# The attention steps of units 8 to 22 moved forward by 0.45 to 0.7 slots in a slot-ordered kernel

## Chip, core and metric

The kernel runs on one core of one Trainium2 chip. The metric is the device time of one execution in microseconds, the median of several runs. The engines in question are TensorE (PE, with its weight loads PEld), VectorE (DVE), ScalarE (ACT) and the DMA queue that SyncE issues (SP). Each works through its own list of instructions in the order in which the program put them there.

## What is computed

Three layers follow each other, for 4 sequences of 768 tokens:

```python
# 1. a linear-attention recurrence, 8 heads of 48
y[:, :, t] = einsum(r[t], state + (u * k[t]) outer v[t])
state = w[t] * state + k[t] outer v[t]
# 2. a dense layer on all 3072 tokens, 384 -> 2048 -> 384
h = x @ w_in
g = h * tanh(softplus(h))
x = g @ w_out
# 3. a greedy gate (8 experts, 384 tokens each), then relu(x @ w1[e]) @ w2[e]
```

## The kernel before

**Tiling.** The recurrence is cut into 24 units (n = 0 to 23); a unit is one chunk of 64 tokens of two sequences, 12 chunks to a pair of sequences. Two units make a group of 256 tokens (g = 0 to 11), and the dense layer works group by group: its first product `mm1` in 8 parts j of 256 hidden columns each (18 matmuls of 256 columns into one of two `Hp` buffers), its second product `mm2` in a stream of small pieces of 3 matmuls.

**Slots.** All work of layers 1 and 2 is a list of events, each with a time in slots, and the program is written out in the sorted order of these times (line 799). There are 96 slots, one `mm1` part to a slot: part j of group g stands at 8g + j + 0.7, and two or three pieces of `mm2` follow at .275 of the next slot. A step of unit n with the offset o stands at 4n - 13 + o (line 737). The offsets come from the table `'u'` of `CFG`, and from `'un'` for single units. The times are no clock: they only decide which instruction stands ahead of which in each engine's list. So four slots, a *half group*, hold one unit, four parts of `mm1` and four stretches of `mm2`.

**Steps of a unit**, with their lines and what they ask of the engines:

- `att0` (390, 393): DVE scan `E`, then the product `rk`.
- `bon1` (422) and `bon2` (428): PE, each followed by a move (`bT`, `bt`) on ACT; `bon2` ends with the DVE product `Dt` (433).
- `inv` (401, 402, 404): ACT table load, Ln and Exp, then DVE `nt`.
- `r1` (412): one DVE product.
- `k1` (439, 442): two DVE instructions that leave the scaled k in the unit's tile `T`.
- `K` (475): four PE transposes of `T`, then the move `kn`. The last chunk of a pair (units 11 and 23) has none.
- `A1` (458, 464): PE products of `T` with `T` and with the state, then the DVE `copy_predicated` (466).
- `S` (493, 500, 502): the new state, on PE and then two or three DVE instructions; none for units 11 and 23, two for unit 12.
- `y` (515, 373, 522): PE, then ACT moves the output to `xg`, and DVE writes its low part. After an odd unit SP packs `xg` with six small DMAs (528); the first `mm1` part of the next group reads them.

**The dense layer's activations**, between the steps: after each `mm1` part ACT reads `Hp` twice (613 `es`, then `hs` by the helper at 373); an `Hp` buffer is free again after `hs`. Twice a group, at the end of a half, ACT runs Arctan (620); 1.6 slots later Sin in two halves q = 0, 1 (630), each followed by a DVE product (631). Sigmoid, Ln/Exp and Sin need three different ACT tables, so every half group has three table loads. On DVE two products `g` (644) follow.

After slot 96 come the gate and the experts, which the change doesn't touch.

Of the kernel before, what the change touches and what calls it, by code (L numbers as in the profile page):

```python
# [25 lines left out]
 'ogT': [7.4, 8.45, 9.9, 10.25, 10.95, 11.85, 12.55, 12.75],  # L26
 'ogM': [8.15, 9.35, 10.2, 10.9, 11.35, 11.95, 12.75, 13.95],
 'u': {'att0': -0.5,
       'bon1': 1.4,
       'bon2': 2.4,  # L30
       'r1': 2.7,
       'k1': 3.175,
       'K': 4.91,
       'A1': 5.52,
       'S': 7.29,
       'y': 7.3,
       'inv': 2.67},
 'un': {0: {'att0': -17.25,
            'inv': -16.75,
            'r1': -16.55,  # L40
# [36 lines left out]
            'y': 6.5},  # L77
        4: {'K': 4.96,
            'A1': 4.82,
            'S': 6.99,  # L80
            'y': 7.0,
            'att0': -0.0,
            'bon1': 0.87,
            'bon2': 3.15,
            'inv': 2.57,
            'r1': 2.6,
            'k1': 3.2},
        5: {'y': 7.46,
            'att0': -1.5,
            'bon1': 2.0,  # L90
            'bon2': 4.6,
# [1 line left out]
            'r1': 3.7,  # L93
            'k1': 4.3,
            'K': 5.9,
            'A1': 6.2,
            'S': 7.45},
        6: {'y': 7.41,
            'K': 5.66,
            'A1': 6.67,  # L100
# [10 lines left out]
            'inv': 2.77,  # L111
            'r1': 2.8,
            'k1': 3.4,
            'K': 5.26,
            'A1': 5.87,
            'S': 7.29,
            'y': 7.3},
        22: {'K': 4.46},
        23: {'K': 4.3, 'A1': 6.0, 'y': 7.1}},
 'rate': [(9, 0), (80, 194), (82, 200), (85, 216), (89, 218), (93, 234), (99, 258)],  # L120
 'close_cv': 15.0,
 'close_att': 86.65,
# [1212 lines left out]
```

## Time and profile before

| | us |
|---|---|
| median of 3 runs | 858.98 (857.58 to 864.3) |
| the profiled execution | 864.1 |
| its span | 862.4 |
| PE busy | 762.9 (88%) |
| PEld busy | 523.1 (61%) |
| DVE busy | 530.4 (62%) |
| ACT busy | 508.6 (59%) |
| PE idle before L610 (`mm1`), of which until a DMA of `xg` / until ACT's `hs` | 34.6, of which 18.4 / 14.4 |

The shares are means over stages: loading and weight conversion up to about 150 us, the steady groups from about 150 to 530 us, the gate until about 645 us, the experts after that. The profile page names for each group of instructions the idle time of its engine just before it and what ended that idle time.

### The profile page before, as it was taken

To read this page: it belongs to the slowest core of one execution; us is meant where nothing else is said; L and a number is where in the kernel's file an instruction comes from. 1 tells how busy PE (TensorE), PEld (TensorE's weight loads), DVE (VectorE), ACT (ScalarE), POOL (GpSimd) and SP (SyncE) were. 2 spreads that over 40 slices of the span, in tenths; PEclk is the share of its full clock that TensorE was granted. 3 is DMA by queue.
4 is the path that set the end of the run, shared out by engine and by line. 5 is a ranking of instruction groups with operands and counts; after the bars stand their busy time and mean duration, and the time that the engine had idled before them with its cause. 6 is when DMAs were issued, how large, how long until landed. Compare 5 with 4: busy or idle time off the path is not lost. (4 is left out here: it accounts for less than half of the span.)

```text
span 862.4 us, 20166 instructions
## 1 busy us (share of the span) xinstructions
PE 762.9 (88%) x8819; PEld 523.1 (61%) x8819; DVE 530.4 (62%) x933; ACT 508.6 (59%) x728; POOL 66.9 (8%) x104
## 2 busy tenths in 40 slices
PE   7774879898898889888899999999959999999996
PEld 4462657576676667666676767555536566555564
DVE  6699885656666767586666642677766533455520
ACT  2349888687887878676778887211005543455521
POOL 1100000000000000000000001000010332222311
PEclk9697889899999999999999999999969999999998
DMA  7860511221232204221221000400244434555200
GB/s 282 235 203 14 148 37 43 49 51 40 52 75 53 56 6 85 51 52 39 53 47 25 11 14 11 165 20 20 55 150 162 141 133 175 189 192 178 71 28 27
DMA packets 22220, 74.12 MB, mean 86 GB/s; under 512 B 4496, under 2 KB 13072, under 8 KB 20080
## 3 DMA queue, kind: packets, MB, share of 16 engines
q1 hardware_dynamic: 19056, 63.35, 25.4%
q0 software_dynamic: 3072, 9.44, 3.5%
q8 instruction: 71, 1.16, 0.6%
q14 instruction: 21, 0.17, 0.1%
HBM read 62.15 MB, written 9.44 MB: 83 GB/s over the span
## 5 line engine op out<-in xcount | busy, mean ns | idle before, releaser
L610 PE MATMUL Hp<-xg,wi 128*128 128x256 f16 x1728 | 214.0, 278 | 34.6 <-DMA xg<-xg 18.4
L658 PE MATMUL X<-wo,g 128*128 128x392 f16 (+1 forms) x1152 | 217.7, 334 | 0.3 <-ACT wT L373 0.3
L610 PEld LDWEIGHTS <-wi 128*128 128x128 f16 x1728 | 167.1, 100 | 69.9 <-issue 26.1
L658 PEld LDWEIGHTS <-g 128*128 128x128 f16 x1152 | 109.5, 99 | 64.9 <-issue 4.5
L1180 PE MATMUL Hp<-xe,a 128*128 128x384 f16 (+1 forms) x612 | 101.0, 317 | 6.4 <-DVE hT L1185 5.2
L613 ACT ACTIVATE es<-Hp 128x512 f32<-128x512 f32 x96 | 58.2, 607 | 80.4 <-PE Hp L610 80.2
L1197 PE MATMUL X<-a,hT 128*128 128x384 f16 x576 | 97.2, 326 | 0.0
L631 DVE TENSOR_TENSOR hs<-hs,es 128x1024 f32<-128x1024 f32 x48 | 56.8, 1222 | 58.7 <-ACT es L630 58.6
L1180 PEld LDWEIGHTS <-a 128*128 128x128 f16 x612 | 57.8, 98 | 48.3 <-issue 14.4
L1197 PEld LDWEIGHTS <-hT 128*128 128x128 f16 x576 | 56.3, 98 | 34.8
L1185 DVE SCALAR_TENSOR_TENSOR hT<-Hp,hT 128x384 f16<-128x384 f32 x64 | 35.4, 554 | 46.8 <-ACT hT L1184 46.8
L1126 DVE SCALAR_TENSOR_TENSOR a<-stg,a 128x1024 f16<-128x1024 f32 (+4 forms) x56 | 59.7, 1067 | 3.2 <-ACT a L1123 2.7
L644 DVE TENSOR_TENSOR g<-hs,g 128x1024 f16<-128x1024 f32 x48 | 58.0, 1244 | 4.8 <-ACT g L373 4.2
L1200 ACT ACTIVATE or<-X 128x384 f32<-128x384 f32 x24 | 11.8, 490 | 81.0 <-issue 60.7
L1123 ACT ACTIVATE a<-stg 128x1024 f16<-128x1024 f32 (+4 forms) x56 | 51.1, 926 | 8.1 <-DMA stg<-in_w_dram 8.1
L373 ACT ACTIVATE hs<-Hp 128x512 f32<-128x512 f32 x91 | 55.3, 608 | 0.0
L630 ACT ACTIVATE es<-es,right 128x1024 f32<-128x1024 f32 x48 | 52.6, 1141 | 0.3
L1184 ACT ACTIVATE hT<-Hp 128x384 f16<-128x384 f32 x64 | 31.4, 490 | 32.9 <-PE Hp L1180 31.8
L1162 DVE SCALAR_TENSOR_TENSOR xe<-cn,xe 128x384 f16<-128x384 f32 x24 | 13.3, 555 | 60.9 <-ACT xe L1161 60.8
L373 ACT ACTIVATE x1o<-X 128x384 f32<-128x384 f32 x19 | 9.4, 495 | 70.0 <-issue 58.5
L620 ACT ACTIVATE es<-es 128x2048 f32<-128x2048 f32 x24 | 46.6, 1940 | 0.1
L1147 POOL DMA_INDIRECT xr<-x_dram,idx x24 | 29.2, 1215 | 114.7 <-DVE idx L1098 106.1
(196 smaller groups left out, 948.3 us busy)
## 6 DMA issues: line engine op xcount, KB each, us to landing
stg<-in_w_dram SPq DMA_DIRECT2D x16, 1536.0 KB, 7.3
T<-in_rkw_dram SPq DMA_DIRECT2D x42, 289.5 KB, 5.0
v<-in_v_dram SPq DMA_DIRECT2D x24, 192.0 KB, 3.4
raw<-in_w_out_dram SPq DMA_DIRECT2D x6, 768.0 KB, 4.8
x_dram<-x1o SPq DMA_DIRECT2D x48, 96.0 KB, 2.2
wo<-in_w_in_dram SPq DMA_DIRECT2D x4, 768.0 KB, 9.4
raw<-in_w_in_dram SPq DMA_DIRECT2D x2, 768.0 KB, 8.3
g<-in_w_in_dram SPq DMA_DIRECT2D x2, 768.0 KB, 11.2
```

The costliest lines, as they stand in the source:

```text
L373: nc.scalar.activation(dst, src, AF.Copy, scale=scale)
L610: nc.tensor.matmul(h[:, fi, :], wi[:, a, kk, f * P:(f + 1) * P], xg[g][:, b, kk, :], start=(n == 0), stop=(n == 3 * KD - 1))
L613: nc.scalar.activation(es[g, hf][:, 2 * q:2 * q + 2, :], h, AF.Sigmoid, scale=-1.0 / (SX * SWI))
L620: nc.scalar.activation(e, e, AF.Arctan)
L630: nc.scalar.activation(e, e, AF.Sin, scale=-2.0, bias=right)
L631: nc.vector.tensor_tensor(h, h, e, op=ALU.mult)
L644: (nc.vector if on_v("glo", 2 * H_ + q) else nc.gpsimd).tensor_tensor(gt[:, 1, sl], h, gt[:, 0, sl], op=ALU.subtract)
L658: nc.tensor.matmul(x, gt[:, a, ff, m * P:(m + 1) * P], wo[:, b, f, 0:n], start=(f == 0 and i == 0), stop=(f == NF - 1 and i == 2))
L1123: nc.scalar.activation(dst[:, 0], src, AF.Copy, scale=sc_)
L1126: nc.vector.scalar_tensor_tensor(dst[:, 1], src, sc_, dst[:, 0], op0=ALU.mult, op1=ALU.subtract)
L1180: nc.tensor.matmul(ps[:, cs], a1[:, a, kk, f * P:(f + 1) * P], x[:, b, kk, cs], start=(n == 0), stop=(n == 3 * KD - 1))
L1197: nc.tensor.matmul(ps, h[:, a, f, ms], a2[:, b, f, :], start=(n == 0), stop=(n == 3 * NF2 - 1))
```

## The change

In the table for all units, nine steps stand 0.45 to 0.7 slots earlier and `att0` stays:

```diff
-       'bon1': 1.4,
-       'bon2': 2.4,
-       'r1': 2.7,
-       'k1': 3.175,
-       'K': 4.91,
-       'A1': 5.52,
-       'S': 7.29,
-       'y': 7.3,
-       'inv': 2.67},
+       'bon1': 0.9,
+       'bon2': 1.9,
+       'r1': 2.25,
+       'k1': 2.7,
+       'K': 4.4,
+       'A1': 5.0,
+       'S': 6.59,
+       'y': 6.6,
+       'inv': 2.2},
```

Units 0 to 7 have tables of their own. Of these, unit 4 has `S` and `y` 0.1 slots earlier, unit 5 `A1` by 0.2 and `S` and `y` by 0.56, unit 7 `K`, `A1`, `S` and `y` by 0.26 to 0.5. Unit 22 loses its own `K` (4.46, now 4.4), unit 23 keeps its own `K` and `A1` (4.2 and 5.0, before 4.3 and 6.0) and takes `y` from the table. Nothing is added or removed: the instructions are the same, in another order. The changed file is one line shorter, so every line number above 115 is one less in it.

What this does to the lists is shown for unit 18 (its tile is `T_88`, its scan `E_134`), in the half group of `mm1` parts 4 to 7 of group 7.

DVE, from unit 18's `nt` on; `hs<-hs,es` are the two Sin products, `S_135` and `xg` belong to unit 17's `S` and `y`, and the next unit's scan follows. Before:

```order
L631 TENSOR_TENSOR hs<-hs,es 128x1024 x2
L404 TENSOR_TENSOR nt<-inv,E_134 128x512
L412 TENSOR_TENSOR T_88<-T_88,E_134 128x512
L439 SCALAR_TENSOR_TENSOR inv<-nt,inv 128x512
L442 SCALAR_TENSOR_TENSOR T_88<-inv,T_88 128x512
L371 TENSOR_SCALAR x1o<-X 128x384
L662 TENSOR_SCALAR V<-X 128x8
L500 TENSOR_TENSOR S_135<-S_138,Y 128x4x48 x2
L502 TENSOR_TENSOR S_135<-S_135,E_137 128x8x48
L522 SCALAR_TENSOR_TENSOR xg<-A,xg 128x4x64 x2
L390 SCALAR_TENSOR_TENSOR E_137<-T_89,first 128x520
```

and after the change:

```order
L403 TENSOR_TENSOR nt<-inv,E_134 128x512
L411 TENSOR_TENSOR T_88<-T_88,E_134 128x512
L630 TENSOR_TENSOR hs<-hs,es 128x1024
L499 TENSOR_TENSOR S_135<-S_138,Y 128x4x48 x2
L501 TENSOR_TENSOR S_135<-S_135,E_137 128x8x48
L521 SCALAR_TENSOR_TENSOR xg<-A,xg 128x4x64 x2
L630 TENSOR_TENSOR hs<-hs,es 128x1024
L438 SCALAR_TENSOR_TENSOR inv<-nt,inv 128x512
L441 SCALAR_TENSOR_TENSOR T_88<-inv,T_88 128x512
L370 TENSOR_SCALAR x1o<-X 128x384
L661 TENSOR_SCALAR V<-X 128x8
L389 SCALAR_TENSOR_TENSOR E_137<-T_89,first 128x520
```

The Sin products moved behind `nt` and `r1`; `S` and the low part of `xg` moved ahead of the second of them, and `k1` of unit 18 (`inv`, then `T_88`) now stands behind all of these.

ACT in the same half, from the move `bt` of unit 18 on; `es<-es,right` are the Sins, `inv` is Ln and Exp, `xg` is unit 17's `y`. Before:

```order
L373 ACTIVATE bt<-Y 128x8
L629 ACT_TABLE_LOAD
L630 ACTIVATE es<-es,right 128x1024 x2
L400 ACT_TABLE_LOAD
L401 ACTIVATE inv<-E_134 128x512
L402 ACTIVATE inv<-inv 128x512
L613 ACT_TABLE_LOAD
L613 ACTIVATE es<-Hp 128x512
L373 ACTIVATE hs<-Hp 128x512
L373 ACTIVATE xg<-A 128x4x128
```

and after the change:

```order
L372 ACTIVATE bt<-Y 128x8
L399 ACT_TABLE_LOAD
L400 ACTIVATE inv<-E_134 128x512
L401 ACTIVATE inv<-inv 128x512
L628 ACT_TABLE_LOAD
L629 ACTIVATE es<-es,right 128x1024
L372 ACTIVATE xg<-A 128x4x128
L629 ACTIVATE es<-es,right 128x1024
L612 ACT_TABLE_LOAD
L612 ACTIVATE es<-Hp 128x512
L372 ACTIVATE hs<-Hp 128x512
```

Ln and Exp moved ahead of the Sins, and the move to `xg` ahead of the second Sin; the table loads are three in both.

PE around the transposes `K` of unit 18, the last matmul ahead of them and the first behind. Before:

```order
L610 LDWEIGHTS wi
L610 MATMUL Hp<-xg,wi 128x256
L475 MATMUL Y<-ident,T_88 128x128 x4
L658 LDWEIGHTS g
L658 MATMUL X<-wo,g 128x392
```

and after the change:

```order
L657 LDWEIGHTS g
L657 MATMUL X<-wo,g 128x392
L474 MATMUL Y<-ident,T_88 128x128 x4
L609 LDWEIGHTS wi
L609 MATMUL Hp<-xg,wi 128x256
```

The transposes moved from behind the half's last `mm1` part to ahead of it, behind the stretch of `mm2` that precedes that part.

## Rows read from the trace of the kernel before

**Rows 1.** Busy time in one whole group: stretch, engines, granted clock, DMA.
```profile
core 0: us, PE busy (x) PEld busy (x) DVE busy (x) ACT busy (x) POOL busy (x), PEclk, DMA share, GB/s
231.70:269.50 37.80, 33.05 (x480) 24.97 (x473) 25.25 (x36) 31.55 (x44) 0.00 (x0) 1.00 0.24 52
```

**Rows 2.** Waits of PE from 150 to 505 us: total, times, longest.
```profile
PE Hp L610 <- DMA xg<-xg: 18.4, 11, 2.9
PE Hp L610 <- ACT hs L373: 14.4, 14, 1.7
PE Y L422 <- DVE rk L393: 2.0, 5, 0.7
```

**Rows 3.** PE in time: start, duration, line, idle before; one half group.
```profile
367.70 2.14 PE L610 MATMUL Hp<-xg,wi 128*128 128x256 f16 x18
...
380.20 2.12 PE L610 MATMUL Hp<-xg,wi 128*128 128x256 f16 x18 [1.18 <-ACT hs L373]
...
382.17 0.60 PE L475 MATMUL Y<-ident,T 128*128 128x128 f32 x4
...
382.60 1.66 PE L658 MATMUL X<-wo,g 128*128 128x392 f16 x9
...
389.04 2.87 PE L610 MATMUL Hp<-xg,wi 128*128 128x256 f16 x18 [2.91 <-DMA xg<-xg]
```

**Rows 4.** ACT in the same half group, same columns.
```profile
369.87 0.60 ACT L613 ACTIVATE es<-Hp 128x512 f32<-128x512 f32 x1 [2.32 <-PE Hp L610]
...
371.47 0.18 ACT L373 ACTIVATE bt<-Y 128x8 f32<-128x8 f32 x1 [1.00 <-PE Y L428]
...
371.67 1.28 ACT L629 ACT_TABLE_LOAD   x1
...
372.96 2.19 ACT L630 ACTIVATE es<-es,right 128x1024 f32<-128x1024 f32 x2
...
376.46 0.63 ACT L401 ACTIVATE inv<-E 128x512 f32<-128x512 f32 x1
...
379.07 0.60 ACT L613 ACTIVATE es<-Hp 128x512 f32<-128x512 f32 x1
...
379.56 0.59 ACT L373 ACTIVATE hs<-Hp 128x512 f32<-128x512 f32 x1
```

**Rows 5.** DVE in the same half group, same columns.
```profile
374.14 2.36 DVE L631 TENSOR_TENSOR hs<-hs,es 128x1024 f32<-128x1024 f32 x2 [1.77 <-ACT es L630]
...
379.00 0.68 DVE L439 SCALAR_TENSOR_TENSOR inv<-nt,inv 128x512 f32<-128x512 f32 x1
...
379.72 0.69 DVE L442 SCALAR_TENSOR_TENSOR T<-inv,T 128x512 f32<-128x512 f32 x1
...
380.87 0.61 DVE L500 TENSOR_TENSOR S<-S,Y 128x192 f32<-128x192 f32 x2
...
381.99 0.75 DVE L522 SCALAR_TENSOR_TENSOR xg<-A,xg 128x256 f16<-128x256 f32 x2
...
382.65 1.23 DVE L390 TENSOR_TENSOR_SCAN E<-T,first 128x520 f32<-128x520 f32 x1
...
383.80 0.66 DVE L393 TENSOR_TENSOR rk<-T 128x512 f32<-128x512 f32 x1
```

**Rows 6.** PE, the transposes of unit 22, same columns.
```profile
461.02 0.66 PE L475 MATMUL Y<-ident,T 128*128 128x128 f32 x4 [0.65 <-DVE S L500]
```

**Rows 7.** 3.4 us behind each PE wait over 1.8 us, columns of rows 1.
```profile
154.90:158.30 3.40, 3.40 (x46) 1.92 (x47) 0.00 (x0) 2.79 (x4) 0.00 (x0) 0.50 0.00 0
165.15:168.55 3.40, 3.40 (x57) 2.60 (x50) 3.33 (x8) 1.88 (x2) 0.00 (x0) 0.50 0.22 65
272.20:275.60 3.40, 3.40 (x27) 2.64 (x27) 0.09 (x1) 1.36 (x4) 0.00 (x0) 1.00 0.93 195
310.45:313.85 3.40, 3.40 (x27) 2.63 (x27) 0.10 (x1) 1.38 (x4) 0.00 (x0) 1.00 0.00 0
349.45:352.85 3.40, 3.40 (x14) 1.85 (x13) 0.00 (x0) 1.08 (x2) 0.00 (x0) 0.50 0.91 193
390.45:393.85 3.40, 3.40 (x15) 1.89 (x13) 0.69 (x1) 0.60 (x1) 0.00 (x0) 0.50 0.33 72
```

More of the change, by code (lines that the diff above doesn't have):

```diff
@@ L79 @@
             'A1': 4.82,
-            'S': 6.99,
-            'y': 7.0,
+            'S': 6.89,
+            'y': 6.9,
             'att0': -0.0,
@@ L87 @@
             'k1': 3.2},
-        5: {'y': 7.46,
+        5: {'y': 6.9,
             'att0': -1.5,
@@ L95 @@
             'K': 5.9,
-            'A1': 6.2,
-            'S': 7.45},
+            'A1': 6.0,
+            'S': 6.89},
         6: {'y': 7.41,
@@ L113 @@
             'k1': 3.4,
[L114 to L119, printed above, removed]
+            'K': 5.0,
+            'A1': 5.4,
+            'S': 6.79,
+            'y': 6.8},
+        23: {'K': 4.2, 'A1': 5.0}},
  'rate': [(9, 0), (80, 194), (82, 200), (85, 216), (89, 218), (93, 234), (99, 258)],
```

## Prediction

> **What bounds the kernel now.** I read the busy time by group first. In a whole group of 37.80 us PE is busy for 33.05, ACT for 31.55 and DVE for 25.25 [rows 1]: PE sets the pace but stands still for some 4 us a group, and ACT has little room behind it. The waits of PE come next [rows 2]. From 150 to 505 us it waits 18.4 us for the packing DMAs of `xg`, at the first `mm1` part of a group, 14.4 us for ACT to free an `Hp` buffer, at the last part of a half group, and 2.0 us for `rk`: 34.8 us together. The timeline of PE, ACT and DVE over one half group then gives the places and durations [rows 3 to 5]; I count time there from the half's first `mm1` part, at 367.70. The last `mm1` part is reached at 11.32 and waits 1.18 for `hs`, and the next group's first part waits 2.91 for `xg` [rows 3]. These two kinds of wait are what the change can win. Last I looked at TensorE's granted clock behind the longest waits: PE waited over 1.8 us six times after 150 us, and behind four of them 3.4 us ran at 0.50, the 1.2 GHz level, though PE was busy throughout; behind the other two the clock stayed at 1.00, which is 2.4 GHz [rows 7]. One such drop costs half of 3.4, 1.7 us.
>
> **The change, step by step.** Nothing is added, so only waits and the clock can move the time.
>
> *`xg` comes early enough.* Follow ACT in the new order. `es` of the half's first part starts 2.17 after that part [rows 3, 4]; successive reads of `Hp` start 0.49 apart, so `bt` follows `hs` at 3.15. From `bt` to the table load is 0.20, the load 1.29, and Ln, Exp and the next load take 2.61 (376.46 to 379.07) [rows 4]. The first Sin starts at 7.25. On DVE its product starts 1.18 later, at 8.43; the two products take 2.36, so one takes 1.18; then come `S`, 1.12 to the low part of `xg`, and that part, 0.75 [rows 5]. It ends at 11.48; before it ended at 382.74, which is 15.04. In the old half 6.30 went from there to the matmul that read the last packed piece. That gives 17.8, and PE comes to the next group no sooner than 19.5 (below). So the 18.4 us go. SP's list is not in the way: the unit load and the `v` load stand ahead of the packing as before.
>
> *`K` comes too early.* The transposes of unit n now stand ahead of the half's last `mm1` part, and they read what `k1` of the same unit writes. What PE does before it reaches them is the same set of matmuls as before it reached that part, so PE is there at 11.32. On DVE `k1` now stands behind the first Sin product, `S`, `xg` and the second Sin product: the latter starts 0.66 after the second half of `xg` was begun (381.99 to 382.65), at 11.39, and takes 1.18; `k1` takes 1.41 (379.00 to 380.41) [rows 5]. `k1` ends at 13.98, where before it ended at 12.71 and was read at 14.47 [rows 3, 5]. So PE stands for 2.7 us, with everything behind the transposes: the last `mm1` part, `bon1`, `A1`, a stretch of `mm2`, the next half. That chain closes on itself, for the next `bt` waits for the next `mm1` part. The wait for `Hp` disappears in it: `hs` would free its buffer at 12.3 (the second Sin ends at 9.9, the table load takes 1.29, `es` and `hs` 1.08). The wait for `rk` disappears too. From 14.0 the transposes (0.43), the part (1.97) and what follows to the next half (3.53, less some rk wait) [rows 3] give the 19.5 used above.
>
> That a transpose placed there does hold PE is seen once: unit 22's stand ahead of the `mm1` part already, and PE waits 0.65 for DVE at them [rows 6]. The Trainium skill ("TensorE: Matmul & The Clock Gate", The mechanism) says that only weight loads may overtake, and that matmuls start and end in program order. By that rule the waiting transposes hold the part behind them, and the trace agrees in the 0.65 us; if matmuls could overtake too, the first rival's time would come out.
>
> *Counting the stalls.* Units 9, 10 and 14 to 22 have the full one: 11 x 2.7 = 29.7. Unit 13 follows a unit whose `S` has one instruction less (about 0.5): 2.2. Unit 12 follows one without `S`: 1.6. At unit 8, `S` and `xg` of unit 7 still stand behind `k1`: 0.9. Unit 11 has no transposes; there the wait for `hs` stays (1.0), and `bon1` waits for `rk`, which ends 1.15 + 0.66 after `k1` [rows 5], at 15.8, instead of 14.3: 1.5. Sum 36.9, against 34.8 removed: **+2.1 us**. The waits that the change was to remove are replaced almost exactly.
>
> *The clock.* Three of the four drops stand behind waits for `xg` and go: -5.1. The one at 165 us is behind another wait and stays. Twelve new stalls of 2.2 us or more come. No row says which of them is followed by a drop: below, none; above, all twelve, 20.4. Four of six waits over 1.8 us were, and the new ones are mostly longer, so I take 8 of 12: **+13.6**.
>
> The Trainium skill ("TensorE: Matmul & The Clock Gate", What's actually happening) puts the cost of running slow until the clock rises at under 1% of a typical kernel's span. By that, an estimate, the drops after 150 us would cost at most 8.6 us here instead of the 15.3 of nine drops, and the sum would be 868. The profile before agrees with it (four drops, 6.8 us); the sum goes by the count of stalls.
>
> *Units 4, 5, 7 and the end.* The earlier `y` of units 5 and 7 serves groups 2 and 3, whose waits are in the 18.4 already. Up to 150 us and in the gate and experts no row lets me expect a change: 0, or a microsecond or two to either side.
>
> **Sum.** 864.1 + 2.1 - 5.1 + 13.6 = 874.7 for the profiled execution. That execution lies 5.1 us above the median of the runs, 858.98. The clock drops that the sum takes away are of the kind that may differ between executions; a median run that has three fewer gives 859.0 + 2.1 + 13.6 = 874.7 as well. Without that, the median would be some 5 us lower. I take 874.
>
> **The rivals.**
>
> *The transposes don't wait (faster).* If `k1` ended by 11.3 instead of 14.0, or if the `mm1` part overtook the waiting transposes, only the waits for `hs` would be left, 12.3 - 11.3 = 1.0 in each of 16 halves. Then 34.8 - 16 = 18.8 us are won, and the three drops: 864.1 - 18.8 - 5.1 = 840. It decides from a lead of 2.7 us on DVE. Against it: four instructions stand in between, and ACT gives the first Sin no sooner than 8.4. For it: unit 22's transposes, placed alike before, waited only 0.65 [rows 6], though there with `k1` ahead of `S` and `xg`. 0.13.
>
> *They wait, but the clock holds.* 864.1 + 2.1 - 5.1 = 861. For it: two of six waits left the clock at 1.00 [rows 7]. Against it: behind the longest wait, the 2.91 us at 389.04 [rows 3], it fell. 0.27.
>
> *More than that.* Every stall is followed by a drop, or DVE, which then has work from 8.4 to beyond 18 without a pause, delays `bon1` and `A1` too: 881 and over. 0.10.
>
> *`xg` is late all the same.* Then a stall would have to be shorter, since both wait in the same chain; it changes the place of the wait, not the time, and is within the forecast.
>
> **How the numbers follow.** Forecast 0.50, at 874; clock holds 0.27, at 861; faster 0.13, at 840; worse 0.10. The range leaves out the fast rival and part of the worst: its low end is 861 less 0.5 us at each of twelve stalls (855), its high end 881 and 2 us (883). A change of 1% is about what a measurement of this kernel can tell from none, 850.4 to 867.6. Faster: the first rival, 0.13. Same: the second and the lower tail of the forecast, 0.33. Slower: 0.54.
>
> **What would show it.** Right: PE's waits for `xg` shrink from 18.4 to under 3, those for `hs` nearly vanish, and a wait of the transposes (line 474 after the change) for DVE's `T` appears, 12 to 14 times, some 2.7 each; half groups of 19.5 us instead of 18.4 without the `xg` wait (389.04 - 2.91 - 367.70); new stretches at 0.50 behind some of them. Wrong: no such wait, or one of under 1 us (then `k1` was earlier than worked out, and the first rival holds); or the waits there, but few stretches at 0.50 (the second). Most fragile is the number of drops, 1.7 us each.

## The result

| | before | after |
|---|---|---|
| median (us) | 860.97 (857.58 to 864.3, 4 runs) | 872.25 (871.41 to 873.53, 4 runs) |
| ratio, 95% interval | 1 | 1.0133 (1.0084 to 1.0181) |
| the profiled execution (us) | 864.1 | 872.8 |
| its span (us) | 862.4 | 871.1 |

The changed kernel is slower by 1.3%. Below are PE's waits from 150 to 520 us, to set beside [rows 2]. Line numbers are one less than in the kernel before, so 474 are the transposes, 421 is `bon1`, 609 `mm1`, and 492 the first product of `S`:

```profile
PE Y L474 <- DVE T L441: 16.5, 7, 2.7
PE Y L474 <- issue: 14.4, 6, 2.7
PE Y L492 <- ACT bt L372: 3.2, 1, 3.2
PE Y L421 <- DVE rk L392: 1.9, 2, 1.2
PE Y L474 <- DVE S L499: 1.5, 1, 1.5
PE Hp L609 <- DMA xg<-xg: 0.6, 1, 0.6
PE Hp L609 <- ACT hs L372: 0.5, 1, 0.5
```

The 18.4 us for `xg` shrank to 0.6 and the 14.4 for `hs` to 0.5. In their place PE stands at the transposes: 16.5 + 14.4 + 1.5 = 32.4 us in 14 places, one for each unit from 8 on that has transposes. ("issue" and "DVE T" are the same wait: the view gives a releaser for seven of these thirteen only, and in the half shown below the transposes labelled "issue" start 0.10 us after `k1` ends.) PE's total wait is what it was, 38.6 us against 38.3 with the wait for `bt` (1.9 before) and the other small ones; it stands elsewhere.

One half group, the one that [rows 3] and [rows 5] show of before, first on PE and then on DVE, with the columns of those rows:

```profile
374.18 2.13 PE L609 MATMUL Hp<-xg,wi 128*128 128x256 f16 x18
...
383.84 1.66 PE L657 MATMUL X<-wo,g 128*128 128x392 f16 x9
...
387.68 0.63 PE L474 MATMUL Y<-ident,T 128*128 128x128 f32 x4 [2.19 <-issue]
...
393.16 2.13 PE L609 MATMUL Hp<-xg,wi 128*128 128x256 f16 x18
```

```profile
380.26 0.69 DVE L411 TENSOR_TENSOR T<-T,E 128x512 f32<-128x512 f32 x1
...
382.11 1.23 DVE L630 TENSOR_TENSOR hs<-hs,es 128x1024 f32<-128x1024 f32 x1 [1.17 <-ACT es L629]
...
383.25 0.61 DVE L499 TENSOR_TENSOR S<-S,Y 128x192 f32<-128x192 f32 x2
...
384.37 0.75 DVE L521 SCALAR_TENSOR_TENSOR xg<-A,xg 128x256 f16<-128x256 f32 x2
...
385.04 1.22 DVE L630 TENSOR_TENSOR hs<-hs,es 128x1024 f32<-128x1024 f32 x1
...
386.17 0.68 DVE L438 SCALAR_TENSOR_TENSOR inv<-nt,inv 128x512 f32<-128x512 f32 x1
...
386.89 0.69 DVE L441 SCALAR_TENSOR_TENSOR T<-inv,T 128x512 f32<-128x512 f32 x1
...
389.19 0.66 DVE L392 TENSOR_TENSOR rk<-T 128x512 f32<-128x512 f32 x1
```

The half starts at 374.18. PE is through with the stretch of `mm2` at 385.49 (387.68 less the 2.19 it waited), 11.31 into the half. `k1` of the unit, the rows at 386.17 and 386.89, ends at 387.58, 13.40 into the half, and the transposes start 0.10 later. On DVE nothing ran between `r1` (380.26) and the first Sin product, which had to wait 1.17 us for ACT; then that product, `S`, the low part of `xg` and the second product all went ahead of `k1`. The half lasts 18.98 (374.18 to 393.16) with no wait for `xg`; in this half DVE moves the first `hs` in ACT's place, so `k1` is 0.5 earlier than in most others. In the halves of units 14 to 17, where ACT moves it, `k1` ends at 13.89 and the stall is 2.7.

The granted clock right behind three of these stalls (columns of [rows 1]):

```profile
226.90:230.20 3.30, 3.30 (x17) 2.36 (x16) 3.25 (x4) 1.02 (x2) 0.00 (x0) 0.50 0.07 15
...
326.70:330.00 3.30, 3.30 (x68) 2.81 (x72) 3.27 (x4) 1.84 (x4) 0.00 (x0) 1.00 0.21 46
...
346.40:349.70 3.30, 3.30 (x18) 2.43 (x17) 3.27 (x5) 0.60 (x1) 0.00 (x0) 0.50 0.08 16
```

The first and the third are at 0.50, with PE busy throughout. In all, ten of the thirteen stalls from 200 to 480 us, each 2.0 to 2.7 us long, have such a stretch behind them (three of the ten begin in the stall's last 0.3 to 0.6 us). With the one at 162 us, behind the wait for `bt`, that makes eleven drops between 150 and 530 us, where before had four [rows 7]. What they come to shows in one long stretch of either kernel, from the first `mm1` part of group 3 to the last `mm1` part of all, before and then after (columns of [rows 1]):

```profile
193.98:530.72 336.74, 303.35 (x4260) 228.41 (x4255) 213.60 (x311) 265.74 (x355) 1.04 (x1) 0.99 0.20 42
...
192.26:539.42 347.16, 313.86 (x4256) 235.48 (x4255) 213.08 (x310) 265.50 (x354) 1.04 (x1) 0.95 0.19 41
```

The stretch takes 347.16 us in place of 336.74. PE stands idle in it for 33.30 us, before for 33.39; it counts as busy for 10.5 us more, with the same work at a mean granted clock of 0.95 in place of 0.99. So the loss lies in the slower clock and not in the waiting. Ahead of this stretch the changed kernel is 1.7 us sooner.

### The profile page after: what moved, and what is told of

It reads as the page before. It is cut to its first block, busy times and chain, and to the rows that moved or that the text cites. A ratio compares the mean times of both kernels' runs of the same rounds, so it can differ in the third digit from the quotient of the medians.

```text
span 871.1 us, 20157 instructions
## 1 busy us (share of the span) xinstructions
PE 768.8 (88%) x8819; PEld 528.5 (61%) x8819; DVE 530.8 (61%) x933; ACT 509.2 (58%) x728; POOL 67.4 (8%) x104
## 5 line engine op out<-in xcount | busy, mean ns | idle before, releaser
L609 PE MATMUL Hp<-xg,wi 128*128 128x256 f16 x1728 | 222.9, 287 | 2.9 <-DVE wi L549 1.7
L657 PE MATMUL X<-wo,g 128*128 128x392 f16 (+1 forms) x1152 | 214.0, 330 | 0.6 <-ACT wT L372 0.6
L609 PEld LDWEIGHTS <-wi 128*128 128x128 f16 x1728 | 175.7, 103 | 39.2 <-DVE wi L549 2.0
L657 PEld LDWEIGHTS <-g 128*128 128x128 f16 x1152 | 107.0, 98 | 63.3 <-issue 1.2
L1196 PEld LDWEIGHTS <-hT 128*128 128x128 f16 x576 | 56.4, 98 | 34.8
L474 PE MATMUL Y<-ident,T 128*128 128x128 f32 x88 | 16.7, 322 | 32.4 <-DVE T L441 16.5
```

The lines of the kernel that those rows point to most:

```text
L609: nc.tensor.matmul(h[:, fi, :], wi[:, a, kk, f * P:(f + 1) * P], xg[g][:, b, kk, :], start=(n == 0), stop=(n == 3 * KD - 1))
L657: nc.tensor.matmul(x, gt[:, a, ff, m * P:(m + 1) * P], wo[:, b, f, 0:n], start=(f == 0 and i == 0), stop=(f == NF - 1 and i == 2))
L1196: nc.tensor.matmul(ps, h[:, a, f, ms], a2[:, b, f, :], start=(n == 0), stop=(n == 3 * NF2 - 1))
```

## The experiments

Each time is given with its ratio to the kernel before, which ran beside it. Its median was 864.61 us beside experiments 1, 2, 4 and 5 and 863.14 beside 3, 6 and 7; the ratio is taken over all runs and is not exactly that of the medians. The changed kernel did not run again beside them, so a difference from its 872.25 us is one between sessions in which the median of before moved by 2 to 4 us (from 860.97).

**What was to be told apart.** My theory was that `K` was put ahead of the `k1` it reads, that PE stands there, and that the clock falls behind the stalls. The rivals: the new order on ACT (Ln and Exp ahead of the Sins) makes the half longer by itself and the transposes only show it; and the drops have another cause, or cost nothing in a chain that waits anyway.

**Experiment 1: `k1` first.** The changed kernel with one number changed:

```diff
-       'k1': 2.7,
+       'k1': 2.47,
```

> The changed kernel with the one step k1 put from 2.7 to 2.47 slots, so that on DVE it stands directly behind r1 and ahead of the first Sin product; K stays at 4.4. Theory: k1 then ends at 8.6 us of the half (Exp ends at 5.9, nt, r1 and k1 take 2.6) and PE comes to the transposes at 11.3 without a wait; hs frees its buffer at 12.3 and PE comes to the last mm1 part at 11.75, a wait of about 0.6 in each half; no drops of the clock in the steady groups. Time 831 us, 826 to 839. Rival (the new order on ACT makes the half longer): 865 to 873 us, with 2 us or more of waits for hs in each half.

Measured: 831.46 us (831.04 to 832.72), ratio 0.9637 (0.9578 to 0.9696). PE's waits, and the same half on DVE and PE:

```profile
PE Hp L609 <- ACT hs L372: 5.4, 9, 1.1
PE Y L421 <- DVE rk L392: 2.9, 6, 1.0
PE Hp L609 <- DMA xg<-xg: 0.4, 1, 0.4
PE Y L474 <- DVE S L499: 0.2, 1, 0.2
```

```profile
354.39 0.69 DVE L411 TENSOR_TENSOR T<-T,E 128x512 f32<-128x512 f32 x1
...
354.99 0.69 DVE L438 SCALAR_TENSOR_TENSOR inv<-nt,inv 128x512 f32<-128x512 f32 x1
...
355.71 0.69 DVE L441 SCALAR_TENSOR_TENSOR T<-inv,T 128x512 f32<-128x512 f32 x1
...
356.32 1.22 DVE L630 TENSOR_TENSOR hs<-hs,es 128x1024 f32<-128x1024 f32 x1
...
359.25 1.22 DVE L630 TENSOR_TENSOR hs<-hs,es 128x1024 f32<-128x1024 f32 x1
...
362.07 0.67 DVE L392 TENSOR_TENSOR rk<-T 128x512 f32<-128x512 f32 x1
```

```profile
359.46 0.60 PE L474 MATMUL Y<-ident,T 128*128 128x128 f32 x4
```

`k1` (354.99 and 355.71) now fills the time in which DVE waited for the first Sin, and the product that follows it at 356.32 starts 1.93 us behind the start of `r1`, where it was 1.85 in the changed kernel. `k1` ends at 356.40, and the transposes at 359.46 don't wait for it. The granted clock doesn't fall any more in the groups:

```profile
170.00:530.00 360.00, 349.01 (x4902) 262.18 (x4892) 241.18 (x372) 296.00 (x397) 3.43 (x17) 1.00 0.23 53
```

All else of the change is kept, Ln and Exp ahead of the Sins too, so the rival on ACT's order falls. The changed kernel's order on DVE costs some 40 us by one misplaced pair of instructions: PE waits 12.9 us in all from 150 to 520 us in place of 38.6, and the ten drops, some 16 us (experiment 4), are gone. With that pair moved the change is a gain of 3.6%: this kernel is faster than both. The waits for `rk`, 2.9 us, had not been foreseen.

**Experiment 2: `K` back.** The changed kernel with `K` behind the half's last `mm1` part again:

```diff
-       'K': 4.4,
+       'K': 4.91,
```

> The changed kernel with the one step K put back to 4.91 slots, behind the last mm1 part of its half group; everything else as changed. Theory (PE stands at the transposes because k1 is late): the transposes are reached at about 14.3 us of the half, after k1 ends at 14.0, so their waits (32 us in the changed kernel) go; what is left is the wait for hs, about 1.0 us in each of 16 halves, and the clock drops behind the stalls go too. Time 837 us, between 833 and 844; PE waits for xg under 3 us in all. Rival (the new order on ACT, Ln and Exp ahead of the Sins, makes the half longer by itself, and the transposes only show it): the wait moves to hs at the last mm1 part, 2 us or more each, and the time stays at 868 to 873 us.

Measured: 854.06 us (852.85 to 855.66), ratio 0.9891 (0.9829 to 0.9954): 1.1% faster than before, but 17 us above what I had expected, and outside its bounds. The waits:

```profile
PE Y L421 <- DVE rk L392: 17.4, 14, 1.8
PE Hp L609 <- ACT hs L372: 12.7, 15, 1.5
```

The waits at the transposes are gone, and so are the drops (the granted clock is 1.00 from 170 to 530 us). Those for `hs` are near the 16 us expected; but 14 waits for `rk` at `bon1` came, one in nearly every half. With one of 3.3 for `bt` PE waits 33.4 us in all, against 38.6 in the changed kernel: most of the 18 us between the two is the clock. PE and DVE in one half:

```profile
379.10 0.43 PE L421 MATMUL Y<-rk,u_T 128*32 128x64 f32 x16 [1.74 <-DVE rk L392]
```

```profile
376.08 0.69 DVE L441 SCALAR_TENSOR_TENSOR T<-inv,T 128x512 f32<-128x512 f32 x1
...
378.38 0.67 DVE L392 TENSOR_TENSOR rk<-T 128x512 f32<-128x512 f32 x1
```

On DVE the next unit's scan and `rk` stand behind `k1`. `k1` ends at 376.77, `rk` at 379.05, and `bon1`, which stands ahead of the transposes in this order, has to wait 1.74. My expectation had followed `k1` to one reader and forgotten the second, behind it in DVE's list.

**Experiment 3: `K` and `bon1` back**, to try that explanation:

```diff
-       'bon1': 0.9,
+       'bon1': 1.4,
...
-       'K': 4.4,
+       'K': 4.91,
```

> The changed kernel with K back at 4.91 and bon1 back at 1.4 slots. With K alone put back PE waited 17.4 us at bon1 for rk, which stands behind the late k1 on DVE, and the time was 854 us. Theory (the late k1 has two readers downstream, the transposes and, through the scan, rk): bon1 now stands behind A1 and a stretch of mm2, at about 17.4 us of the half, after rk at 15.8; only the waits for hs remain, about 1.0 us in each of 16 halves: 838 us, 834 to 844, waits for rk under 3 us. Rival (the half can't be shorter than about 19 us in the new order on ACT): 850 us or more, with the wait at another place.

Measured: 836.22 us (835.45 to 837.58), ratio 0.97 (0.9648 to 0.9751).

```profile
PE Hp L609 <- ACT hs L372: 12.3, 15, 1.5
PE Hp L609 <- DMA xg<-xg: 2.1, 3, 0.8
```

No wait for `rk` is left in that view, and those for `hs` are most of what remains, 12.3 of some 19 us. The late `k1` has two readers; with both moved back on PE, the change is a gain.

**Experiment 4: the clock.** The changed kernel with idle matmuls ahead of the transposes; they write into the transposes' own tile and are overwritten:

```diff
             t = pq.tile([P, NP, C], F32, name="Y", bufs=2)
+            if n >= 9:
+                for _ in range(8):
+                    nc.tensor.matmul(t.rearrange("p a c -> p (a c)"), id16, warm_rhs, start=True, stop=True)
             for p in range(NP):
                 nc.tensor.transpose(t[:, p, :], k1[:, p, :], ident)
```

> The changed kernel with 8 idle matmuls of 512 columns (1.7 us, a constant times the scan's start tile, written into the transposes' own PSUM tile and overwritten by them) ahead of the transposes of units 9 to 22: the stall stays, for k1 comes no sooner, but PE is busy in two thirds of it. Theory (the drops of the granted clock come from the stalls): the waits at the transposes shrink to about 1 us, the half groups keep their 19.5 us, and the ten drops between 200 and 480 us go: 872 - 17 = 855 us, 852 to 859. Rival (the drops have another cause, or cost nothing since the chain waits anyway): 869 to 876 us.

Measured: 856.35 us (854.63 to 857.57), ratio 0.9916 (0.9886 to 0.9946). The waits (the transposes are line 477 here), one half on PE, and the granted clock in three stretches over the groups:

```profile
PE Y L477 <- DVE T L441: 7.7, 13, 0.9
PE Y L477 <- DVE S L502: 1.5, 1, 1.5
```

```profile
374.46 1.89 PE L475 MATMUL Y<-first,id 128*128 128x512 f16 x8
...
376.77 0.66 PE L477 MATMUL Y<-ident,T 128*128 128x128 f32 x4 [0.42 <-DVE T L441]
```

```profile
215.00:300.00 85.00, 81.37 (x1132) 60.12 (x1129) 57.98 (x86) 72.67 (x97) 0.00 (x0) 1.00 0.27 54
300.00:380.00 80.00, 76.86 (x1103) 56.83 (x1105) 55.24 (x83) 61.71 (x84) 1.04 (x1) 1.00 0.23 51
380.00:460.00 80.00, 77.74 (x1163) 57.36 (x1153) 55.63 (x83) 62.67 (x86) 0.00 (x0) 1.00 0.19 43
```

The idle matmuls (374.46) take 1.89 us of the stall and 0.42 is left; `k1` comes no sooner. The granted clock is 1.00 from 215 to 460 us. The kernel does strictly more than the changed one and takes 15.9 us less (872.25 to 856.35): ten drops, 1.6 us each. The halves show it one by one. From 192 to 499 us of the changed kernel there are fifteen, each from its first `mm1` part to the next half's. The ten with a drop are 1.5 to 1.7 us longer than the same halves here, 16.3 in all; the other five, three of them with a stall of 2.2 to 2.7 us, differ by 0.3 at most. So the drops come from PE standing still in the stalls, and they cost time; the rival falls. What is then left against before is a ratio a little under 1, 7 to 8 us, most of which are the three drops that before has behind its waits for `xg` (1.7 each) and this kernel has not: without the clock the exchange of waits is about even.

**Experiment 5: `K` alone.** The kernel before with `K` at 4.4:

```diff
-       'K': 4.91,
+       'K': 4.4,
```

> The kernel before with the one step K put to 4.4 slots, ahead of the last mm1 part; nothing else is changed. Theory: k1 ends at 12.7 us of the half as before, PE comes to the transposes at 11.3 and waits about 1.4 us there in place of the 1.2 us for hs; the half gets 0.2 to 0.4 us longer, half of which is taken back from the wait for xg. Time 863 us, 860 to 867; waits of the transposes for DVE in 12 to 14 places of 1.2 to 1.5 us; waits for xg still 13 to 18 us. Rival (an early K is harmful by itself, whatever k1 does): 868 us or more.

Measured: 864.37 us (858.47 to 871.24, 10 runs), ratio 0.9999 (0.9962 to 1.0036).

```profile
PE Y L475 <- DVE S L500: 18.5, 12, 2.3
PE Hp L610 <- DMA xg<-xg: 15.5, 10, 2.3
PE Y L475 <- DVE T L442: 1.9, 1, 1.9
PE Hp L610 <- ACT hs L373: 0.7, 1, 0.7
```

The waits at the transposes came, 22.1 us of them (18.5 + 1.9 + 1.7, the third not shown), those for `hs` went to 0.7, those for `xg` to 15.5. Most end with the first addition of `S` (500), not with `k1`: in this order `S` stands right behind `k1`, and the transposes also need the buffer that it reads. So the stalls are 1.6 us in the mean, near the 1.4 expected, though the wait that ends last is not the one expected. PE waits 42.6 us in all, 4.3 more than before, with one drop fewer. An early `K` by itself does no harm that can be measured in the time; it is `K` early and `k1` late together.

**Experiment 6: `y` alone.** The kernel before with `S` and `y` moved, nothing else:

```diff
-       'S': 7.29,
-       'y': 7.3,
+       'S': 6.59,
+       'y': 6.6,
```

> The kernel before with S at 6.59 and y at 6.6 slots in the table for all units, and nothing else of the change. Theory (the move of y is the useful part, the stall at the transposes the harm): the low part of xg ends at about 9.5 us of the half instead of 15.0, so the 18 us of waits for xg and the clock drops behind them go; ACT has the move to xg ahead of es and hs, so hs frees its buffer 0.5 us later, 8 us over 16 halves. Time 861 - 18 - 5 + 8 = 846 us, 840 to 852; no wait of the transposes over 0.7 us. Rival (the waits for xg hide behind others and come back as waits for hs): 858 us or more.

Measured: 848.72 us (844.15 to 850.45), ratio 0.9825 (0.9765 to 0.9885).

```profile
PE Hp L610 <- ACT hs L373: 16.6, 14, 2.1
PE Hp L610 <- DMA xg<-xg: 5.4, 4, 2.1
```

The waits for `xg` fall from 18.4 to 5.4 and those for `hs` grow by 2.2, less than the 8 expected; why was not tried. The trace still has three drops of the clock between 150 and 530 us, at 154, 165 and 264, one fewer than before where three fewer were expected. PE waits 25.0 us in all from 150 to 520 us in place of 38.3; that and one drop are 15 us, near the 14 measured. The move of `y` is a useful part of the change, but not all of it: the whole change with `k1` first (experiment 1) is 17 us faster still. Which of the other moves gives that was not tried.

**Experiment 7: `k1` second.** The changed kernel with `k1` behind the first Sin product and ahead of `S`:

```diff
-       'k1': 2.7,
+       'k1': 2.5,
```

> The changed kernel with k1 put from 2.7 to 2.5 slots: on DVE behind the first Sin product and ahead of S and xg, one place later than with 2.47. Theory: k1 ends at 11.0 us of the half, just ahead of PE at the transposes (11.3), so they don't wait; but S and the low part of xg are 1.4 us later, 12.9, and 6.3 us on, at 19.2, the last packed piece arrives 1.3 to 1.7 us after PE asks for it: the wait for xg is back in some 8 groups. Time 831 + 11 = 842 us, 836 to 848. Rival (the place of k1 relative to S and xg is of no weight as long as the transposes don't wait): 830 to 834 us.

Measured: 847.74 us (846.61 to 847.9), ratio 0.9832 (0.9781 to 0.9883). The time is within its bounds, but not for the reason given:

```profile
PE Y L421 <- DVE rk L392: 16.4, 14, 1.7
PE Hp L609 <- ACT hs L372: 4.0, 9, 0.7
PE Hp L609 <- DMA xg<-xg: 0.6, 1, 0.6
```

The wait for `xg` did not come back. PE waits 16.4 us for `rk` instead, as in experiment 2, which makes the halves so long that `xg` is in time. The pair takes its 1.4 us from DVE's full stretch behind the first Sin product, and everything up to `rk` ends as late as in the changed kernel: in the half that starts at 357.50 here,

```profile
372.50 0.67 DVE L392 TENSOR_TENSOR rk<-T 128x512 f32<-128x512 f32 x1
```

`rk` ends 15.67 into the half, as it does in the half of the changed kernel shown above (389.85 less 374.18). One place earlier (experiment 1) the pair lies in DVE's idle time and costs next to nothing: 16 us between two neighbouring places.

## Why the prediction was right, point by point

- **Direction and size.** Forecast 874 from 858.98, a ratio of 1.0175; measured 872.25, 1.0133 (1.0084 to 1.0181). The profiled execution rose by 8.7 us, where the sum had 10.6. That is nearer than the terms were, and in part luck. The waits gave +0.3 in place of +2.1, and ten drops came in place of eight; with the three that went (-5.1) and 1.6 us for each new one the terms as measured add up to 11.2, and where the 2.5 us down to 8.7 went is open. That a median run of before has three drops fewer than the profiled one was not shown, for only one execution was traced. The granted clocks on record go with it (0.963 in a run of 858.2 us, 0.952 in one of 867.44).
- **`xg` comes early enough.** Right: 18.4 became 0.6.
- **`K` comes too early.** Right in place and mechanism. `k1` was put at 13.98 for a half in which ACT reads `hs`; it came at 13.89 in most such halves, and at 13.40 in the half shown, where DVE reads it. PE's arrival was put at 11.32 and was 11.31. The stalls were up to 2.72, and for eleven units I had taken 2.7 for all; they sum to 26.8 instead of 29.7, because units 9, 10, 18, 19 and 22 waited about 2.2 and 20 and 21 about 2.5. At 18 and 19 `k1` came sooner; at the others PE came later, for instance at 11.81 for unit 10, with 27 matmuls of `mm2` ahead of the transposes in place of 24, and at 11.73 for unit 22, with four matmuls of the gate (line 696) besides.
- **The count of stalls.** Forecast 36.9 against 34.8 removed; measured 32.4 at the transposes, 1.9 for `rk` and 0.5 for `hs`, 34.8. With every wait counted, that for `bt` too, which the prediction left out, it is 38.6 against 38.3. So the exchange was even, where I had +2.1.
- **The clock.** The largest term and the weakest in the prediction. Eight new drops were forecast and ten came, at 1.6 us each in experiment 4 against the 1.7 worked out. That the stalls would be followed by drops was right; how many was a guess from four in six, and nothing in the rows gave it. The Trainium skill ("TensorE: Matmul & The Clock Gate", What's actually happening) says of the ramp to the faster clock that its penalty is under 1% of a typical kernel's span. The eleven drops here, at 1.6 to 1.7 us each, are some 2% of the span, so for stalls that recur the measurement decides against that figure, and the sum by it (868) was too low.
- **The rivals.** The price of the fast one, 840, does not follow from its conditions. With the wait at the transposes taken away and `k1` as late as in the changed kernel, the time is 854 (experiment 2); with `k1` at 10.48 into the half, just ahead of PE, it is 848 (experiment 7). In both `rk` is late, which the price left out. With `k1` ahead of the first Sin product it is 831 (experiment 1), for there the waits for `hs` come to 5.4 and not 16. The rival in which the stalls stay and the clock holds was priced at 861; experiment 4, the nearest to it, gives 856.
- **What stays open.** Why three of thirteen stalls (2.2, 2.7 and 2.2 us, no shorter than the others) had no drop behind them was not tried.

## What to carry to other kernels

When a producer and its reader are both moved earlier in a list, follow the producer through its engine's own list: it may have become later while its reader came sooner, and a second reader further down the same list, here `rk`, waits for it as well. Look for the idle time that the engine has anyway, in front of an instruction that waits for another engine, and put the producer there: the same pair of instructions cost next to nothing in that place and 16 us one place further. A stall of the matrix engine is worth more than its length when the granted clock falls behind it; counting these drops in the trace of before gave the sign of this change, since the waits came out even.

## What was not expected of the hardware

Waits of 2.0 to 2.7 us were enough for the clock to fall to its 1.2 GHz level behind ten of thirteen, and 1.89 us of matmuls with no use inside the same waits kept it at 2.4 GHz and made the kernel 15.9 us faster, though no useful instruction came sooner by them.
